# Strided PV between the local transposes, shared V rows and a result copy on ScalarE, and half sums of layer 1 among local PV

## The chip, the cores and the metric

One core of one Trainium2 chip. The metric is device time in microseconds (us). A profile of one execution goes with each kernel; its span starts a little later than the timed interval, so 332.4 in the trace belongs to 334.2 timed. Engines: PE (TensorE, matmuls), PEld (its weight loads), DVE (VectorE), ACT (ScalarE), POOL (GpSimd).

## The reference

```python
# attention: batch 8, heads 8, seq 576, head_dim 64
mask_local   = (rel >= 0) & (rel < 32)                          # heads 0-3
mask_strided = (rel >= 0) & (pos[None, :] % 32 == pos[:, None] % 32)   # heads 4-7
attn = softmax(where(mask, q @ k.T / 8, -1e9)); attn_out = attn @ v
x = attn_out.transpose(0, 2, 1, 3).reshape(4608, 512)
h = x @ w_in                                                    # 512 -> 2048, "layer 1"
g = maximum(h, 0) + alpha * minimum(h, 0)
out = g @ w_out                                                 # 2048 -> 512, "layer 2"
```

## The kernel before

The heads are handled in pairs: two strided and two local pairs per batch. For each unit of two pairs, `T` transposes q or k on PE and copies the result on DVE and ACT; `Sc` makes scores and their exponentials (ACT); `Pv` multiplies by V, takes a reciprocal and a product on DVE; `X` transposes the result and copies it to `xT`, layer 1's input. Layer 1 makes 16 blocks of 128 columns per 512 tokens; each block is 4 matmuls into a buffer in PSUM, the memory that matmuls write to (3 buffers in turn), a negative part on ACT and `gT` on DVE, which frees the buffer. Batches 0 and 1 are fed first, in a fixed order; batch 0 alone, with filler matmuls on a zero tile between pieces, meant to keep the PE clock up, batch 1 between pieces of layer 2.

```python
    def over_v(b, eng):                      # the 32 V rows that neighbouring blocks share
        v16 = vls[b % 2]
        cast_copy(eng, v16[0:32, 1:24, :], v16[96:128, 0:23, :])

    def alone(u0, u1, ahead):                # u0: strided unit, u1: local unit
        A, L = (2 * u0, 2 * u0 + 1), (2 * u1, 2 * u1 + 1)
        # ... T(u0,q) T(u0,k), four Sc of A, T(u1,q) T(u1,k), two Sc of L[0],
        #     six Pv of A, two Sc of L[1], X(A[0]) X(A[1]),
        #     over_v on DVE, four Pv of L, X(L[0]) X(L[1])        (cut to its order)

    def lin1_piece(n, m):
        # ...
        hps = phpool.tile([128, 512], F32, tag="hps", name="hps")
        for kk in range(4):                  # kk 0, 1: local pairs; kk 2, 3: strided pairs
            # ... matmul(hps, win16[:, kk, block m], xT[:, kk, tokens])
        neg = npool.tile([128, 512], F32, tag="neg", name="neg")
        keep(nc.scalar.activation(neg, hps, AF.Relu, scale=-1.0))
        def fin():
            keep(nc.vector.scalar_tensor_tensor(
                gTs[n][:, m, :], neg, oma[:, m : m + 1], hps, op0=ALU.mult, op1=ALU.add))
        late.append(fin)
```

The softmax here doesn't subtract the row's maximum and nothing guards it: scores larger than these inputs give would overflow.

Of the kernel before, what the change touches and what calls it, by code (L numbers as in the profile page):

```python
# [9 lines left out]
F32 = mybir.dt.float32  # L10
# [21 lines left out]
def kernel(  # L32
# [10 lines left out]
    nc = tc.nc  # L43
    keep = tc.keep_in_program_order

    B, H, S, D = q.shape
# [17 lines left out]
    phpool = ctx.enter_context(tc.tile_pool(name="ph", bufs=3, space=bass.MemoryType.PSUM))  # L64
    pbpool = ctx.enter_context(tc.tile_pool(name="pb", bufs=1, space=bass.MemoryType.PSUM))
# [4 lines left out]
            name=nc.get_next_instruction_name(), act_func_set_id=6, ins=[], outs=[]  # L70
# [10 lines left out]
    win16 = cpool.tile([128, 4, 2048], F16)  # L81
    wout16 = cpool.tile([128, 16, 512], F16)
    xT = cpool.tile([128, 4, RING], F16)
# [89 lines left out]
    def cast_copy(eng, o, i):  # L173
        if eng == "act":
            keep(nc.scalar.copy(o, i))  # L175
        elif eng == "dve":
            keep(nc.vector.tensor_copy(o, i))  # L177
        else:
            keep(nc.gpsimd.tensor_copy(o, i))  # L179

    def cast_v(b, pr, eng):

        v16 = vss[b % 2]
        cast_copy(eng, v16[0:72, 2 * pr : 2 * pr + 2, :, 0:64],
                  loaded[b][0:72, 1024 * pr : 1024 * pr + 1024].rearrange(
                      "p (h t d) -> p h t d", h=2, t=8))
        cast16[(b, True, "v")] = v16

    def over_v(b, eng):

        v16 = vls[b % 2]
        cast_copy(eng, v16[0:32, 1:24, :], v16[96:128, 0:23, :])
# [7 lines left out]
    NEARLY = 2  # L200

    def make_pair(g):
        P = Pair()
        P.g, P.b, P.hp = g, g // 4, g % 4
        P.strided = P.hp >= 2
        P.pr = P.hp % 2
        P.n, P.w = (8, 72) if P.strided else (6, 96)
        u = g // 2
        P.dx = P.b >= DX and P.strided
        P.xd = P.b >= DX and P.hp < 3  # L210
        if P.dx:
            P.qT, P.kT = (z[u % 2].rearrange("r e c -> r (e c)") for z in (qTs, kTs))
        else:
            P.qT, P.kT = qTs[u % 2][:, g % 2], kTs[u % 2][:, g % 2]
        P.sgroups = ([0, 1, 2, 3], [4, 5, 6, 7]) if P.strided else ([0, 1, 2], [3, 4, 5])
        P.pgroups = ([0, 1, 2], [3, 4, 5], [6, 7]) if P.strided else P.sgroups
        P.et = {}
        P.x16 = None
        return P
# [111 lines left out]
    def pv_piece(P, a):  # L331
        if P.x16 is None:
            if P.xd and P.strided:
                P.x16 = x16s
            else:
                P.x16 = xpool.tile([128, 1024], F16, tag="x16", name="x16")
        v16 = cast16[(P.b, P.strided, "v")]
        grp = P.pgroups[a]
        r = 72 if P.strided else 128
        pv = pspool.tile([128, 512], F32, tag="ps", name="pv")  # L340
        nb = 2 * len(grp)
        for x in range(nb):
            t, hh = grp[x // 2], x % 2
            et, c = P.et[(t, hh)]
            keep(nc.tensor.matmul(  # L345
                pv[:, 65 * x : 65 * x + 65], et[0:r, c : c + 128],
                v16[0:r, 2 * P.pr + hh, t, :] if P.strided else v16[:, 6 * (2 * P.pr + hh) + t, :],
                start=(x == 0), stop=(x == nb - 1), skip_group_check=True))
        w = P.w
        rc = rpool.tile([128, 8], F32, tag="rc", name="rc")  # L350
        pvv = pv[0:w, 0 : 65 * nb].rearrange("r (c e) -> r c e", e=65)
        keep(nc.vector.reciprocal(rc[0:w, 0:nb], pvv[:, :, 64]))  # L352
        c0 = 128 * grp[0]
        keep(nc.vector.tensor_tensor(  # L354
            P.x16[0:w, c0 : c0 + 64 * nb].rearrange("r (c e) -> r c e", e=64),
            pvv[:, :, 0:64],
            rc[0:w, 0:nb].unsqueeze(2).to_broadcast([w, nb, 64]), op=ALU.mult))

    def x_piece(P):
        xp = pspool.tile([128, 1024], F16, tag="ps", name="xp")  # L360
        for t in range(P.n):
            keep(nc.tensor.transpose(  # L362
                xp[:, P.w * t : P.w * t + P.w], P.x16[0 : P.w, 128 * t : 128 * t + 128], ident[0 : P.w, 0 : P.w]))
        base = (P.b % 4) * S
        if P.strided:
            keep(nc.scalar.copy(  # L366
                xT[:, P.hp, base : base + S].rearrange("r (p t) -> r p t", t=8),
                xp[:, 0:576].rearrange("r (t p) -> r p t", t=8)))
        else:
            keep(nc.vector.tensor_copy(xT[:, P.hp, base : base + S], xp[:, 0:576]))  # L370

    def x_dma(P):
        base = (P.b % 4) * S
# [14 lines left out]
    pairs = [make_pair(g) for g in range(npair)]  # L388
    pieces = []

    def feed(fn, g):
        pieces.append((g, fn))

    def T(u, nm):
        return lambda: transpose_piece(u, nm)

    def Sc(g, i):
        return lambda: score_piece(pairs[g], i)

    def Pv(g, i):  # L400
        return lambda: pv_piece(pairs[g], i)

    def X(g):
        return lambda: x_piece(pairs[g])

    def alone(u0, u1, ahead):

        A, L = (2 * u0, 2 * u0 + 1), (2 * u1, 2 * u1 + 1)
        feed(T(u0, "q"), -1)
        feed(T(u0, "k"), -1)  # L410
        for g in A:
            for i in range(2):
                feed(Sc(g, i), -1)
        if ahead:
            feed(T(u1, "q"), -1)
            feed(T(u1, "k"), -1)
            for i in range(2):
                feed(Sc(L[0], i), -1)
        for g in A:
            for i in range(3):  # L420
                feed(Pv(g, i), -1)
        if not ahead:
            feed(T(u1, "q"), -1)
            feed(X(A[0]), -1)
            feed(T(u1, "k"), -1)
            feed(X(A[1]), -1)
            for i in range(2):
                feed(Sc(L[0], i), -1)
        for i in range(2):
            feed(Sc(L[1], i), -1)  # L430
        if ahead:
            for g in A:
                feed(X(g), -1)
        for g in L:
            for i in range(2):
                if g == L[0] and i == 0:
                    feed(lambda: (over_v(u0 // 2, "dve"), pv_piece(pairs[L[0]], 0)), -1)
                else:
                    feed(Pv(g, i), -1)
        for g in L:  # L440
            feed(X(g), -1)

    alone(1, 0, True)
    end0 = len(pieces)
    alone(3, 2, True)
    end1 = len(pieces)


# [75 lines left out]
    def attn_step(end):  # L524
        if pos["i"] < end:
            pieces[pos["i"]][1]()
            pos["i"] += 1
        while late:
            late.pop(0)()


    gTs = {}

    def lin1_piece(n, m):
        if m == 0:
            gTs[n] = gpool.tile([128, 16, 512], F16, tag="gT", name="gT")
        c0 = (512 * n) % RING
        parts = [(c0, 0, min(512, RING - c0))]
        if c0 + 512 > RING:
            parts.append((0, RING - c0, 512 - (RING - c0)))  # L540
        hps = phpool.tile([128, 512], F32, tag="hps", name="hps")
        for kk in range(4):
            for x, (src, dst, w) in enumerate(parts):
                keep(nc.tensor.matmul(  # L544
                    hps[:, dst : dst + w],
                    win16[:, kk, 128 * m : 128 * m + 128],
                    xT[:, kk, src : src + w],
                    start=(kk == 0 and x == 0),
                    stop=(kk == 3 and x == len(parts) - 1),
                    skip_group_check=True,  # L550
# [9 lines that stand above are left out]
# [45 lines left out]
    def warm(n):  # L605

        for _ in range(n):
            keep(nc.tensor.matmul(wps, wrm[:, 0:128], wrm, start=True, stop=True))  # L608
# [54 lines left out]
    for i in range(end0):  # L663
        if i == 1:
            keep(nc.tensor.transpose(apt[:, 0:16], alpha_r, id16))
            keep(nc.vector.tensor_scalar(
                oma, apt[:, 0:16], -1.0, 1.0, op0=ALU.mult, op1=ALU.add))
        if i == 4:
            cast_v(0, 0, "dve")
            cast_v(0, 1, "dve")  # L670
        attn_step(end0)
        if i < 2:
            warm(4)
        else:
            warm(1)

    def attn_n(n, end):
# [78 lines left out]
```

## Time and profile before

| | before |
|---|---|
| time, median (lowest to highest of 6) | 334.18 us (333.87 to 334.32) |
| first local PV on PE, batch 0 / batch 1 | 23.02 / 61.38 us |
| layer 1 resumes after batch 0 / batch 1 (both inputs there) | 27.16 / 66.59 us |
| layer 1 of the first tokens ends, layer 2 begins | 40.75 us |
| copy of the shared V rows | DVE, 0.54 us |

Times in the middle rows are positions in the trace. The prediction shows the lines they come from. PE is 96% busy, so what counts is when PE gets its next input. The two handovers from attention to layer 1 are the places where it has to wait.

### The profile page before, as it was taken

The page shows a single profiled execution, that of the slowest core. Times are in us where ns is not written, and L with a number is a line of the kernel's source. Part 1 is how long each engine was busy: PE and PEld are TensorE (multiplying, and loading weights), DVE is VectorE, ACT ScalarE, POOL GpSimd, SP SyncE. Part 2 cuts the span into 40 slices and gives each one's busy share as a digit, 9 for nine tenths or more (in the row PEclk, how much of TensorE's full clock was granted, in tenths as well). Part 3 has the DMA queues.
Part 4 walks back from the last instruction along what each step waited for, and adds up shares of the span by engine and source line. Part 5 has one row for each costly group of instructions (what it writes and reads, how often), then busy time and mean ns, then how long its engine had stood idle before and what let it go on. Part 6 is the DMA issues. An engine that isn't in the chain of part 4 may idle for free.

```text
span 332.4 us, 6351 instructions
## 1 busy us (share of the span) xinstructions
PE 320.5 (96%) x2533; PEld 163.2 (49%) x2533; DVE 185.1 (56%) x363; ACT 172.5 (52%) x300; POOL 142.2 (43%) x154
## 2 busy tenths in 40 slices
PE   6899999999999999999999999999999999999995
PEld 2554455554554444444558754445444444444444
DVE  5477836477553873387428833784368337605800
ACT  2644753467535744575457644773476336425611
POOL 7932497137679365736483528332611400000000
PEclk9999999999999999999999999999999999999999
DMA  6999999399398649683979295715530120011011
GB/s 220 191 207 207 236 210 194 85 245 157 66 87 125 200 59 147 114 234 40 154 138 221 25 153 109 133 13 109 129 67 20 49 85 33 0 65 63 0 63 65
DMA packets 73117, 39.22 MB, mean 118 GB/s; under 512 B 54064, under 2 KB 64768, under 8 KB 73088
## 3 DMA queue, kind: packets, MB, share of 16 engines
q0 software_dynamic: 41760, 17.38, 48.7%
q1 hardware_dynamic: 31328, 21.44, 26.0%
q8 instruction: 20, 0.33, 0.4%
q14 instruction: 9, 0.07, 0.1%
HBM read 38.01 MB, written 9.44 MB: 143 GB/s over the span
## 4 chain that ended last, share of the span: by engine, by line
PE 89%; DVE 4%; ACT 3%; DMA 2%; issue 1%; SPq 0%; ACTq 0%
PE ops L586 37%; PE hps L544 36%; PE pv L345 4%; PE sp L295 4%; PE tp L235 3%; DMA ql<-in_q_dram 2%; DVE x L354 1%; PE wps L608 1%; PE ops L577 1%; ACT xT L366 1%; DVE qT L177 1%; ACT osb L591 1%; PE sp L311 1%; PE sph L311 1%; PE xp L362 1%
## 5 line engine op out<-in xcount | busy, mean ns | idle before, releaser
L586 PE MATMUL ops<-wout,gT 128*128 128x512 f16 x560 | 136.9, 379 | 0.2 <-DVE gT L557 0.2
L544 PE MATMUL hps<-xT,win 128*128 128x512 f16 (+1 forms) x640 | 134.3, 358 | 2.5 <-ACT xT L366 2.0
L557 DVE SCALAR_TENSOR_TENSOR gT<-neg,oma,hps 128x512 f16<-128x512 f32 x144 | 106.0, 744 | 49.8 <-ACT neg L554 42.2
L554 ACT ACTIVATE neg<-hps 128x512 f32<-128x512 f32 x144 | 86.0, 597 | 46.4 <-PE hps L544 45.2
L329 POOL TENSOR_TENSOR et<-et,consts 128x576 f16<-128x576 f16 (+1 forms) x48 | 61.1, 1274 | 95.4 <-ACT et L319 95.3
L544 PEld LDWEIGHTS <-win 128*128 128x128 f16 x640 | 59.4, 98 | 59.4 <-issue 6.1
L586 PEld LDWEIGHTS <-gT 128*128 128x128 f16 x560 | 48.3, 97 | 46.3 <-issue 0.5
L319 ACT ACTIVATE et<-sp 72x576 f16<-72x576 f32 (+1 forms) x56 | 36.1, 645 | 29.2 <-PE sp L295 15.3
L591 ACT COPY osb<-ops 128x512 f32<-128x512 f32 x35 | 20.5, 585 | 53.4 <-PE ops L586 49.6
L352 DVE RECIPROCAL rc<-pv 72x6 f32<-72x6 f32 (+2 forms) x80 | 14.9, 186 | 55.7 <-PE pv L345 55.6
L354 DVE TENSOR_TENSOR x<-pv,rc 96x384 f16<-96x384 f32 (+2 forms) x65 | 34.5, 531 | 2.2
L345 PEld LDWEIGHTS <-et 72*128 72x128 f16 (+1 forms) x448 | 23.4, 98 | 16.5 <-DVE x L354 1.1
L295 PEld LDWEIGHTS <-kT 64*128 64x128 f16 x448 | 10.8, 95 | 26.5 <-issue 21.2
L295 PE MATMUL sp<-qT,kT 64*128 64x72 f16 (+1 forms) x392 | 16.9, 201 | 1.9 <-ACT kT L175 1.7
L177 DVE COPY qT<-tp 128x1024 f16<-128x1024 f16 (+1 forms) x11 | 11.3, 1030 | 12.3 <-PE tp L235 12.3
L608 PE MATMUL wps<-wrm 128*128 128x512 f16 x44 | 15.7, 428 | 1.2 <-DVE wrm L620 1.2
L167 POOL DMA_DIRECT2D vl<-in_v_dram x8 | 11.1, 1394 | 10.7 <-PE xp L362 9.1
L345 PE MATMUL pv<-vs,et 72*128 72x65 f16 x256 | 15.3, 194 | 0.1
L179 POOL COPY vs<-stv 72x1024 f16<-72x1024 f16 x14 | 14.3, 1032 | 0.0
L175 ACT COPY kT<-tp 128x1024 f16<-128x1024 f16 (+1 forms) x11 | 9.4, 858 | 8.4 <-PE tp L235 8.4
L345 PE MATMUL pv<-vl,et 128*128 128x65 f16 x192 | 11.1, 194 | 0.0
L383 ACT COPY xT<-xs 128x576 f16<-128x576 f16 x5 | 6.5, 1301 | 5.2 <-DMA xs<-x16s 5.2
(73 smaller groups left out, 169.5 us busy)
## 6 DMA issues: line engine op xcount, KB each, us to landing
out_dram<-osb SPq DMA_DIRECT2D x35, 256.0 KB, 2.3
ql<-in_q_dram SPq DMA_DIRECT2D x6, 512.0 KB, 5.5
kl<-in_k_dram SPq DMA_DIRECT2D x6, 512.0 KB, 6.6
stv<-in_v_dram POOLq DMA_DIRECT2D x8, 288.0 KB, 6.2
vl<-in_v_dram POOLq DMA_DIRECT2D x6, 384.0 KB, 9.8
win<-in_moe_w_in_dram POOLq DMA_DIRECT2D x4, 512.0 KB, 10.1
wout<-in_moe_w_out_dram POOLq DMA_DIRECT2D x4, 512.0 KB, 17.1
ql<-in_q_dram POOLq DMA_DIRECT2D x3, 512.0 KB, 8.9
```

Source lines behind the costliest of these rows:

```text
L295: keep(nc.tensor.matmul(sps[y][:, w * x : w * x + w], P.kT[hf, k0 : k0 + 128], P.qT[hf, q0 : q0 + w], start=(x == 0), stop=(x == len(grp) ...
L319: keep(nc.scalar.activation(ev.rearrange("r (y c) -> r y c", y=2), sp[0:r, :, 0:n], AF.Exp, scale=SCALE))
L329: keep(nc.gpsimd.tensor_tensor(ev, ev, m, op=ALU.mult))
L345: keep(nc.tensor.matmul(pv[:, 65 * x : 65 * x + 65], et[0:r, c : c + 128], v16[0:r, 2 * P.pr + hh, t, :] if P.strided else v16[:, 6 * (2 * ...
L352: keep(nc.vector.reciprocal(rc[0:w, 0:nb], pvv[:, :, 64]))
L354: keep(nc.vector.tensor_tensor(P.x16[0:w, c0 : c0 + 64 * nb].rearrange("r (c e) -> r c e", e=64), pvv[:, :, 0:64], rc[0:w, 0:nb].unsqueeze ...
L544: keep(nc.tensor.matmul(hps[:, dst : dst + w], win16[:, kk, 128 * m : 128 * m + 128], xT[:, kk, src : src + w], start=(kk == 0 and x == 0) ...
L554: keep(nc.scalar.activation(neg, hps, AF.Relu, scale=-1.0))
L557: keep(nc.vector.scalar_tensor_tensor(gTs[n][:, m, :], neg, oma[:, m : m + 1], hps, op0=ALU.mult, op1=ALU.add))
L586: keep(nc.tensor.matmul(ops, gTs[n][:, kf, 128 * mt : 128 * mt + 128], wout16[:, kf, :], start=(kf == 0), stop=(kf == 15)))
L591: keep(nc.scalar.copy(osb, ops))
L608: keep(nc.tensor.matmul(wps, wrm[:, 0:128], wrm, start=True, stop=True))
```

## The change

Its intent, read from the diff: fill the wait for the local transposes with strided PV; relieve DVE, which works without pause before the local part, by giving ACT the V rows and one result copy; and replace filler by useful work, the kk 2 and 3 halves of five layer 1 blocks ("half sums" below).

```diff
-            keep(nc.vector.tensor_copy(xT[:, P.hp, base : base + S], xp[:, 0:576]))
+            cast_copy("act" if P.b < NEARLY and P.hp == 0 else "dve",
+                      xT[:, P.hp, base : base + S], xp[:, 0:576])
 ...
+        fns += [Pv(A[0], 0), T(u1, "q"), Pv(A[0], 1), T(u1, "k"), Pv(A[0], 2), Sc(L[0], 0), Sc(L[0], 1)]
+        fns += [Pv(A[1], 0), Pv(A[1], 1), Sc(L[1], 0), Pv(A[1], 2), Sc(L[1], 1), X(A[0]), X(A[1])]
+        fns += [lambda: (over_v(u0 // 2, "act"), pv_piece(pairs[L[0]], 0)), Pv(L[0], 1)]
+        fns += pre[0:2] + [Pv(L[1], 0)] + pre[2:3] + [Pv(L[1], 1)] + pre[3:] + [X(L[0]), X(L[1])]
 ...
+    def lin1_pre(m):
+        if m == 3:
+            sp = pbpool.tile([128, 2, 512], F32, tag="sp", name="hps4")
+            pre[3], pre[4] = sp[:, 0], sp[:, 1]
+        else:
+            pre[m] = phpool.tile([128, 512], F32, tag="hps", name="hps")
+        for z in ((3, 4) if m == 3 else (m,)):
+            for kk in (2, 3):
+                keep(nc.tensor.matmul(pre[z], ..., start=(kk == 2), stop=False, ...))
 ...   # lin1_piece: where a half sum is ready, only kk 0 and 1 are added;
 ...   # filler stops once half sums have begun (both cut)
```

More of the change, by code (lines that the diff above doesn't have):

```diff
@@ L404, in X, with alone @@
         return lambda: x_piece(pairs[g])
-    def alone(u0, u1, ahead):
+    def alone(u0, u1, pre):
         A, L = (2 * u0, 2 * u0 + 1), (2 * u1, 2 * u1 + 1)
-        feed(T(u0, "q"), -1)
-        feed(T(u0, "k"), -1)
-        for g in A:
-            for i in range(2):
-                feed(Sc(g, i), -1)
-        if ahead:
-            feed(T(u1, "q"), -1)
-            feed(T(u1, "k"), -1)
-            for i in range(2):
-                feed(Sc(L[0], i), -1)
-        for g in A:
-            for i in range(3):
-                feed(Pv(g, i), -1)
-        if not ahead:
-            feed(T(u1, "q"), -1)
-            feed(X(A[0]), -1)
-            feed(T(u1, "k"), -1)
-            feed(X(A[1]), -1)
-            for i in range(2):
-                feed(Sc(L[0], i), -1)
-        for i in range(2):
-            feed(Sc(L[1], i), -1)
-        if ahead:
-            for g in A:
-                feed(X(g), -1)
-        for g in L:
-            for i in range(2):
-                if g == L[0] and i == 0:
-                    feed(lambda: (over_v(u0 // 2, "dve"), pv_piece(pairs[L[0]], 0)), -1)
-                else:
-                    feed(Pv(g, i), -1)
-        for g in L:
-            feed(X(g), -1)
-    alone(1, 0, True)
+        fns = [T(u0, "q"), T(u0, "k")] + [Sc(g, i) for g in A for i in range(2)]
+        fns += [Pv(A[0], 0), T(u1, "q"), Pv(A[0], 1), T(u1, "k"), Pv(A[0], 2), Sc(L[0], 0), Sc(L[0], 1)]
+        fns += [Pv(A[1], 0), Pv(A[1], 1), Sc(L[1], 0), Pv(A[1], 2), Sc(L[1], 1), X(A[0]), X(A[1])]
+        fns += [lambda: (over_v(u0 // 2, "act"), pv_piece(pairs[L[0]], 0)), Pv(L[0], 1)]
+        fns += pre[0:2] + [Pv(L[1], 0)] + pre[2:3] + [Pv(L[1], 1)] + pre[3:] + [X(L[0]), X(L[1])]
+        for fn in fns:
+            feed(fn, -1)
+    alone(1, 0, [lambda m=m: lin1_pre(m) for m in range(4)])
     end0 = len(pieces)
-    alone(3, 2, True)
+    alone(3, 2, [])
     end1 = len(pieces)
@@ L532 @@
     gTs = {}
+    pre = {}
+    def lin1_pre(m):
[6 more added lines that the diff above has]
+            for kk in (2, 3):
+                keep(nc.tensor.matmul(
+                    pre[z], win16[:, kk, 128 * z : 128 * z + 128], xT[:, kk, 0:512],
+                    start=(kk == 2), stop=False, skip_group_check=True))
     def lin1_piece(n, m):
@@ L540, in lin1_piece @@
             parts.append((0, RING - c0, 512 - (RING - c0)))
-        hps = phpool.tile([128, 512], F32, tag="hps", name="hps")
-        for kk in range(4):
+        ready = n == 0 and m in pre
+        hps = pre[m] if ready else phpool.tile([128, 512], F32, tag="hps", name="hps")
+        if ready:
+            for z in ((3, 4) if m == 3 else () if m == 4 else (m,)):
+                for kk in (0, 1):
+                    keep(nc.tensor.matmul(
+                        pre[z], win16[:, kk, 128 * z : 128 * z + 128], xT[:, kk, 0:512],
+                        start=False, stop=(kk == 1), skip_group_check=True))
+        for kk in () if ready else range(4):
             for x, (src, dst, w) in enumerate(parts):
@@ L673 @@
             warm(4)
-        else:
+        elif not pre:
             warm(1)
```

## The prediction

> **What bounds the kernel now.** I read the page first (busy shares, chain of waits), then the busy time by stage, then the chain in order of time, then the timelines of PE, ACT and DVE up to 66 us, since the change touches nothing later.
>
> ```profile
> PE 320.5 (96%) x2533; PEld 163.2 (49%) x2533; DVE 185.1 (56%) x363; ACT 172.5 (52%) x300; POOL 142.2 (43%) x154
> ...
> PE 89%; DVE 4%; ACT 3%; DMA 2%; issue 1%; SPq 0%; ACTq 0%
> ```
>
> PE is the bound: 96% busy and 89% of the chain. The rest of the chain lies mostly in the attention of batches 0 and 1, where PE hands over to DVE and ACT and back. By stage (stretch in us, its length, then busy time of each engine with instruction counts):
>
> ```profile
> 13.50:26.67 13.17, 11.61 (x157) 6.85 (x156) 9.20 (x27) 5.75 (x13) 6.14 (x12) 1.00 1.43 193
> 26.67:40.75 14.08, 13.97 (x66) 6.24 (x64) 10.93 (x16) 8.96 (x15) 4.45 (x7) 1.00 1.24 217
> 40.75:66.10 25.35, 23.96 (x259) 13.39 (x258) 12.33 (x32) 11.66 (x26) 15.92 (x20) 1.00 1.25 167
> 66.10:105.20 39.10, 38.69 (x351) 19.92 (x351) 24.43 (x48) 22.44 (x40) 26.67 (x27) 1.00 0.85 138
> ```
>
> Stage A (13.5 to 26.7) is batch 0's attention; much of its PE time is filler on a zero tile, so 11.61 busy is no bound there. Stage B (26.7 to 40.75) is layer 1 of the first tokens, 64 matmuls back to back. Stage C (to 66.1) is batch 1's attention threaded into layer 2. From 66 us on PE is 99% busy (38.69 of 39.10), so a microsecond gained or lost before 66 us should reach the end unchanged. The chain (start, length, what):
>
> ```profile
> 25.69 0.56 DVE x L354
> 26.64 0.47 DVE xT L370
> 27.16 13.76 PE hps L544 x63
> 40.91 1.73 PE ops L586 x8
> ...
> 65.13 0.56 DVE x L354
> 66.08 0.47 DVE xT L370
> 66.59 5.12 PE hps L544 x23
> ```
>
> A and C both end on the same hand-over: normalise the last local PV, transpose it, copy xT, and only then layer 1 resumes, at 27.16 and 66.59. These two times are what the change must pull in. What precedes the first, on DVE and ACT (start, length, instruction, idle before):
>
> ```profile
> 22.00 0.54 DVE L177 COPY vl<-vl 32x1495 f16<-32x1495 f16 x1
> 23.40 0.19 DVE L352 RECIPROCAL rc<-pv 96x6 f32<-96x6 f32 x1 [0.85 <-PE pv L345]
> ...
> 21.98 0.71 ACT L316 ACTIVATE et<-sph 128x288 f16<-128x288 f32 x2
> 22.57 1.19 ACT L366 COPY xT<-xp 128x576 f16<-128x576 f16 x2
> 28.00 0.60 ACT L554 ACTIVATE neg<-hps 128x512 f32<-128x512 f32 x1 [4.24 <-PE hps L544]
> ```
>
> The V rows shared between blocks cost 0.54 us on DVE and are ready at 22.54, before local PV starts on PE (23.02). ACT then idles 4.24 us, which is the slack the change aims at. But ACT comes free for that work only about 23.7, after exponentials and two xT copies.
>
> **What the Trainium skill says.** (1) "ScalarE: Activation LUTs", section "What ACT_TABLE_LOAD costs": an ACTIVATE with immediate scale and bias takes 186 ns + 0.833 ns per element, and neighbours overlap by about 93 ns. The trace agrees for copies too: kT 128x512 590 ns, the 128x1024 cast 1045 ns (the formula gives 613 and 1039). For the 1495 columns of V I estimate 0.186 + 1495 x 0.000833 = 1.43 us. (2) The same page's "Rules for kernel authors" calls VectorE up to about 3x faster per element on 16-bit single-source work; the trace has 0.54 on DVE, so 2.6x by this estimate. (3) "PSUM — Partial Sum Buffer", section "PSUM bank collisions raise a hardware error": two engines must not touch one bank in the same quadrant at once, and by bank is the simple guard. In the trace ACT's copy of one half of tp starts only when DVE's copy of the other half has ended (14.29 + 0.69, then 15.01). (4) "TensorE: Matmul & The Clock Gate", Part 1: PE falls to half clock after an idle window of about 3.4 us. The trace has clock 1.00 throughout these stages, and its longest PE pause there is 0.90 us.
>
> **The change part by part.** I walk each engine's queue of the changed program in order with durations and starts of the old trace. Steps used: strided PV of 6 matmuls to its reciprocal 0.38 (17.65 to 18.03), reciprocal plus product 0.70 (18.03 to 18.73), filler 0.22, score piece 0.49, eight transposes 0.45, 128x512 matmul 0.216 (13.76 / 63 is 0.218), about 0.05 from a finish to its waiter.
>
> *Strided PV between the local transposes.* Old: six strided PVs from 17.65, and DVE works without pause from 18.03 to 22.54. New: the first PV goes at 13.64, right after the strided scores, and fills DVE's and ACT's wait for the local transposes. The price: the transposes' copies alternate with the products on DVE (x 14.25, qT 14.72, then ACT's qT 15.45, kT 15.93 to 16.52), so local scores start at 16.84, not 16.14. Then PVs and scores alternate at PE's own pace: local scores 16.84, 17.64, 19.24, 20.38; strided transposes 21.09 and 21.57; the first local PV stands at PE's head at 22.05 instead of 23.02. Gain 0.97.
>
> *V rows on ACT.* In ACT's queue this copy stands behind the last exponential (21.06 to 21.77) and both xT copies (21.65 to 22.84). It starts near 22.72 and ends near 24.15. The first matmul of local PV doesn't need it, the second does: 24.2. PE stands 2.1 us. Gain of 0.97 has become a loss of 1.18 (24.2 against 23.02).
>
> *Half sums of five blocks.* Ten matmuls (2.16 us) move out of stage B to between the four local PVs, where filler stood. They also spread the PVs: 24.2, 24.57, 25.83, 26.44. The last product ends at 27.69, the last transposes end at PE 28.0, xT of the first local pair is on ACT (27.93 to 28.5) beside DVE's (28.19 to 28.66). Layer 1's second halves start at 28.55 and have both inputs at about 28.77, against 27.16: 1.61 late, less the 2.16 already done.
>
> *What follows in stage B.* Five blocks are complete 2.16 us after the start, while ACT (0.60) and then DVE (0.75, pitch about 0.67) take them one by one: gT 0 starts 29.80, then 30.47, 31.14, 31.81 (ends 32.56). Blocks 3 and 4 share one two-bank tile, and in the changed program ACT's negative part of block 4 waits for DVE's gT of block 3, although they lie in two banks. So block 4 goes 32.59 on ACT, 33.22 on DVE, gT 5 from 33.89 to 34.64. PE has blocks 5, 6, 7 done at 33.3, and block 8 needs the buffer of block 5: it starts 34.69, a stop of 1.4. Blocks 8 to 15 take 8 x 0.864 = 6.9: end 41.6 instead of 40.75. Sum up to here: 1.61 - 2.16 + 1.4 = +0.85.
>
> *Stage C*, on the old clock. The order is the same without half sums. The interleaving saves the two pauses around the local transposes (old 0.47 before the scores at 51.58) and little else: the first local PV stands ready at 61.15, not 61.38. But ACT's queue there is xT (59.35 to 59.95), the layer 2 result copy (60.2 to 60.8), xT (to 61.3), V rows (61.2 to 62.65). PE stands from 61.15 to 62.7. Three layer 2 pieces and PVs later the last PV is at 65.8; old it was at 64.52 with layer 1 resuming 2.07 later. So 67.87 instead of 66.59: +1.28.
>
> Sum: 0.85 + 1.28 = +2.1 us, so 334.2 + 2.1 = 336.3.
>
> **The rivals.** (a) *The intended gain.* If V rows were ready by 22.0 and 61.1 (ACT's copy cheap, or its queue earlier than I walk), stage A would end 2.1 sooner and C 1.5 sooner: about 332.7. For it: ACT idles 4.24 us there in total. Against: the queue order puts exponentials and xT copies ahead, and nothing at 1495 columns on ACT can be near 0.5 us when 512 take 0.59. (b) *Nothing shows:* the half sums give 2.16 and the wait on ACT takes it, with DVE keeping up in stage B: without the 1.4 stop the time is 334.9. For it: DVE is busy only 10.93 of 14.08 there. Against: in bursts it isn't the average that counts, with three buffers. (c) *The clock.* Filler ends once half sums begin, and PE has pauses of 2.1, 1.4 and 1.5 us. If that were idle enough to halve the clock for a window, another 1.7 to 3.4 would be lost: 338 to 340. Against: each pause is under 3.4 us.
>
> **Range and chances.** Most of my error is in the two waits for V rows (1.43 us is estimated, no such copy ran on ACT) and in the stop in stage B. Halving both V waits gives 334.5, all of them longer by 0.5 with a spell of lower clock gives 338.5. Range 334.0 to 338.3. Two per cent is 6.7 us, more than any sum of these: faster 0.01, within 0.96, slower 0.03.
>
> **What would show each step.** Right: ACT's vl copy at 1.4 us, ending near 24.2 and near 63.5 (62.65 plus the 0.85); PE idle before PV on vl of about 2 and 1.5 us, released by ACT; layer 1's second halves from about 28.6; block 4's ACT step starting after block 3's gT; PE waiting over 1 us for a gT near 33 to 35; layer 1 of the next tokens resuming near 68.7. Wrong: a vl copy under 0.9 us, local PV starting before 23 us, no PE idle among the layer 1 blocks, or PE clock below 1.00 in stages A to C.

## The result and the profile after

The changed kernel took 336.65 us (median of 6, 336.41 to 338.34) against 334.18: ratio 1.0081, 95% interval 1.0061 to 1.0102, so 0.8% slower. Ratios here are the mean time of one kernel's fast runs over that of the other's of the same rounds, so not quite the ratio of the medians.

PE of the changed kernel in batch 0 and layer 1 (start, length, instruction, count, and the idle time before it with what ended it):

```profile
22.06 0.19 PE L345 MATMUL pv<-vl,et 128*128 128x65 f16 x1
24.32 0.31 PE L345 MATMUL pv<-vl,et 128*128 128x65 f16 x5 [2.06 <-ACT vl L175]
...
28.75 2.32 PE L536 MATMUL hps<-xT,win 128*128 128x512 f16 x10 [0.47 <-ACT xT L175]
30.91 2.75 PE L541 MATMUL hps<-xT,win 128*128 128x512 f16 x12
34.85 7.07 PE L541 MATMUL hps<-xT,win 128*128 128x512 f16 x32 [1.19 <-DVE gT L554]
41.76 1.89 PE L583 MATMUL ops<-wout,gT 128*128 128x512 f16 x8
```

Local PV arrives 0.96 us earlier than before (22.06 against 23.02) and is then stopped after one matmul. The second matmul is the first that reads the shared rows, and it waits for ACT. Later PE stops once more, between the block 7 and block 8 matmuls, for a gT. ACT in the same kernel shows why the rows are late:

```profile
21.02 0.71 ACT L316 ACTIVATE et<-sph 128x288 f16<-128x288 f32 x2 [0.37 <-PE sph L311]
21.62 1.19 ACT L366 COPY xT<-xp 128x576 f16<-128x576 f16 x2
22.83 1.43 ACT L175 COPY vl<-vl 32x1495 f16<-32x1495 f16 x1
...
31.11 0.60 ACT L551 ACTIVATE neg<-hps 128x512 f32<-128x512 f32 x1 [0.15 <-PE hps L536]
32.77 2.07 ACT L551 ACTIVATE neg<-hps 128x512 f32<-128x512 f32 x4 [1.06 <-DVE gT L554]
...
61.30 0.59 ACT L588 COPY osb<-ops 128x512 f32<-128x512 f32 x1 [0.23 <-PE ops L583]
61.78 0.65 ACT L366 COPY xT<-xp 128x576 f16<-128x576 f16 x1
62.31 1.43 ACT L175 COPY vl<-vl 32x1495 f16<-32x1495 f16 x1
```

The V copy takes 1.43 us, and it starts only when the exponential and two xT copies ahead of it are through. In batch 1 a layer 2 result copy stands ahead too. Begun that late, the copy's length counts nearly in full: it starts 0.58 us after PE's first matmul ended (22.06 + 0.19) in batch 0, and 0.10 before that in batch 1 (62.22 + 0.19), so 1.43 of the first pause and all of the second are the copy itself. The line at 32.77 is block 4's negative part, which waited 1.06 us for block 3's gT; the two blocks are the two halves of one tile, `hps4`. DVE, in turn, waited for it:

```profile
30.01 2.72 DVE L554 SCALAR_TENSOR_TENSOR gT<-neg,oma,hps 128x512 f16<-128x512 f32 x4 [1.24 <-ACT neg L551]
33.40 2.72 DVE L554 SCALAR_TENSOR_TENSOR gT<-neg,oma,hps 128x512 f16<-128x512 f32 x4 [0.66 <-ACT neg L551]
```

PE in batch 1 of the changed kernel:

```profile
62.22 0.19 PE L345 MATMUL pv<-vl,et 128*128 128x65 f16 x1
63.79 0.31 PE L345 MATMUL pv<-vl,et 128*128 128x65 f16 x5 [1.37 <-ACT vl L175]
...
68.97 3.40 PE L541 MATMUL hps<-xT,win 128*128 128x512 f16 x15 [0.28 <-DVE xT L177]
```

Layer 1 resumes at 68.97 instead of 66.59, which is 2.38 late; the span is 334.8 instead of 332.4, which is 2.4 longer. So everything was lost before 69 us and nothing after. The page of the whole execution sums the two pauses in one row (busy time, mean ns of one, idle before and its releaser), first before, then after:

```profile
L345 PE MATMUL pv<-vl,et 128*128 128x65 f16 x192 | 11.1, 194 | 0.0
```

```profile
L345 PE MATMUL pv<-vl,et 128*128 128x65 f16 x192 | 11.4, 194 | 3.4 <-ACT vl L175 3.4
```

### The profile page after: what moved, and what is told of

Read it like the earlier page. It is cut to its first block, busy times and chain, and to the rows that moved or that the text cites. A ratio compares the mean times of both kernels' runs of the same rounds, so it can differ in the third digit from the quotient of the medians.

```text
span 334.8 us, 6345 instructions
## 1 busy us (share of the span) xinstructions
PE 320.1 (96%) x2529; PEld 163.8 (49%) x2529; DVE 183.4 (55%) x359; ACT 176.2 (53%) x304; POOL 142.1 (42%) x154
## 4 chain that ended last, share of the span: by engine, by line
PE 75%; ACT 3%; DVE 2%; issue 1%; ACTq 0%
PE ops L583 34%; PE hps L541 32%; PE pv L345 3%; PE sp L295 3%; PE tp L235 2%; PE ops L574 1%; ACT xT L366 1%; ACT osb L588 1%; DVE gT L554 1%; ACT vl L175 0%; DVE qT L177 0%; DVE x L354 0%; PE xp L362 0%; ACT neg L551 0%; PE tt L263 0%
## 5 line engine op out<-in xcount | busy, mean ns | idle before, releaser
L541 PE MATMUL hps<-xT,win 128*128 128x512 f16 (+1 forms) x620 | 130.0, 357 | 3.6 <-ACT xT L366 2.0
L541 PEld LDWEIGHTS <-win 128*128 128x128 f16 x620 | 57.5, 98 | 58.2 <-issue 7.2
L345 PEld LDWEIGHTS <-et 72*128 72x128 f16 (+1 forms) x448 | 24.3, 98 | 20.4 <-issue 3.6
L605 PE MATMUL wps<-wrm 128*128 128x512 f16 x40 | 14.9, 455 | 1.2 <-DVE wrm L617 1.2
```

Of the source, the lines that this page charges most:

```text
L345: keep(nc.tensor.matmul(pv[:, 65 * x : 65 * x + 65], et[0:r, c : c + 128], v16[0:r, 2 * P.pr + hh, t, :] if P.strided else v16[:, 6 * (2 * ...
L541: keep(nc.tensor.matmul(hps[:, dst : dst + w], win16[:, kk, 128 * m : 128 * m + 128], xT[:, kk, src : src + w], start=(kk == 0 and x == 0) ...
L605: keep(nc.tensor.matmul(wps, wrm[:, 0:128], wrm, start=True, stop=True))
```

## The experiments

The main theory: PE stands for the V rows because of their place in ACT's queue (2.06 and 1.37 us), and part of the half sums' gain is lost to a stop of layer 1 for a buffer. The rivals: the new order of PV itself delays the local part; DVE or ACT is overloaded as a whole; the PE clock drops. All kernels gave correct results. Three groups ran on three chips, each with runs of the kernel before in the same rounds (medians 334.16, 334.22, 334.16).

| run | us, median (range) | ratio to before (95% interval) |
|---|---|---|
| e1 V rows on DVE | 332.75 (332.43 to 332.99) | 0.9957 (0.9945 to 0.9969) |
| e2 V rows on ACT, earlier | 332.92 (332.64 to 333.04) | 0.9962 (0.9950 to 0.9974) |
| e3 no half sums | 337.44 (336.93 to 337.67) | 1.0101 (1.0087 to 1.0116) |
| e4 block 4's negative part early | 337.62 (336.12 to 337.93) | 1.0093 (1.0076 to 1.0110) |
| e5 before, V rows on ACT | 338.11 (337.97 to 338.54) | 1.0118 (1.0105 to 1.0132) |
| e6 before, new order alone | 333.10 (332.97 to 333.13) | 0.9966 (0.9953 to 0.9980) |
| e7 e1 and e4 together | 332.28 (332.21 to 332.41) | 0.9943 (0.9930 to 0.9955) |
| e8 e4 with filler in the pause | 336.14 (336.11 to 336.31) | 1.0058 (1.0046 to 1.0071) |
| e9 e1 with four half sums | 332.04 (331.66 to 332.37) | 0.9933 (0.9920 to 0.9947) |
| e10 e7, result copy on DVE | 332.59 (332.29 to 332.69) | 0.9950 (0.9938 to 0.9963) |
| e11 e4 again | 336.15 (336.06 to 336.48) | 1.0062 (1.0049 to 1.0074) |
| e12 e8 again | 336.07 (336.06 to 336.16) | 1.0057 (1.0044 to 1.0070) |

All lie within 2% of before. The intervals separate kernels with the late V rows from those without; among e1, e2, e6, e7, e9 and e10 they overlap in part, and differences there lean on the traces.

### e1: V rows back on DVE

```diff
-        fns += [lambda: (over_v(u0 // 2, "act"), pv_piece(pairs[L[0]], 0)), Pv(L[0], 1)]
+        fns += [lambda: (over_v(u0 // 2, "dve"), pv_piece(pairs[L[0]], 0)), Pv(L[0], 1)]
```

> The changed kernel with only the copy of the shared V rows back on DVE. Theory A (PE stood for that copy in ACT's queue, 2.06 us in batch 0 and 1.37 us in batch 1): both pauses go, everything behind them moves up, time 336.65 - 2.2 - 1.5 = 332.9, below the kernel before (334.2). DVE is idle there (3.75 and 4.79 us before the first local reciprocal), so the 0.54 us copy should not show on it. Rival B (the new order of strided PV and local transposes itself delays the local part, and the V rows only fill that delay): under 1 us is won, 335.7 or more. Rival C (DVE becomes the bound again, as the change's author feared): 335 to 336, with a new DVE wait before local PV.

Measured 332.75, 3.9 below the changed kernel and 1.4 below before. The V copy on DVE and PE of this kernel:

```profile
20.94 0.54 DVE L177 COPY vl<-vl 32x1495 f16<-32x1495 f16 x1
...
22.06 0.34 PE L345 MATMUL pv<-vl,et 128*128 128x65 f16 x6
...
26.53 2.32 PE L536 MATMUL hps<-xT,win 128*128 128x512 f16 x10 [0.47 <-ACT xT L175]
28.68 2.75 PE L541 MATMUL hps<-xT,win 128*128 128x512 f16 x12
32.64 7.07 PE L541 MATMUL hps<-xT,win 128*128 128x512 f16 x32 [1.20 <-DVE gT L554]
...
65.22 5.12 PE L541 MATMUL hps<-xT,win 128*128 128x512 f16 x23 [0.27 <-DVE xT L177]
```

The six matmuls run through, and all that follows is 2.2 us earlier; the stop at block 8 is unchanged, so it is a cost of its own. The copy took its 0.54 us on DVE at 20.94, ahead of need. After batch 1 layer 1 resumes at 65.22 instead of 68.97, 3.75 earlier, and the two profiled runs differ by 3.76 (336.69 and 332.93). Rivals B and C fall.

### e2: V rows on ACT, but earlier in its queue

```diff
-... Pv(A[1], 0), Pv(A[1], 1), ... lambda: (over_v(u0 // 2, "act"), pv_piece(pairs[L[0]], 0)) ...
+... lambda: (pv_piece(pairs[A[1]], 0), over_v(u0 // 2, "act")), Pv(A[1], 1), ... Pv(L[0], 0) ...
```

> The changed kernel with the V rows still on ACT, but issued earlier in ACT's queue: behind the first strided PV of the second pair, where ACT is idle from 18.92 to 20.00 and from 56.5 to 57.8. Theory A (the place in the queue costs, not the engine or its 1.43 us): as on DVE, 332.9 to 333.3, no PE pause before local PV, perhaps 0.2 us of delay of one exponential. Rival (ACT's total load is what costs, since ACT got 3.7 us more work): no gain, about 336.6.

Measured 332.92, as on DVE. ACT of this kernel:

```profile
18.64 1.43 ACT L175 COPY vl<-vl 32x1495 f16<-32x1495 f16 x1
19.98 0.64 ACT L319 ACTIVATE et<-sp 128x576 f16<-128x576 f32 x1
```

The same 1.43 us on the same engine, ended by 20.1. So in a good place neither the engine nor the length costs anything. The place is what made the 1.43 us count: emitted at its consumer, the copy sits behind everything that ACT was given before. What a shorter copy would cost in that late place was not run.

### e3: no half sums

```diff
-    alone(1, 0, [lambda m=m: lin1_pre(m) for m in range(4)])
+    alone(1, 0, [])
```

> The changed kernel without the half sums of layer 1 (filler stays in their place; V rows and one result copy still on ACT). Theory A: the 2.16 us of PE work moved ahead is nearly all given back, because the half sums spread the local PVs (layer 1's start moves from about 28.9 to 28.4 without them) and because layer 1 then stops 1.2 us for a buffer; layer 1 would end near 42.05 instead of 41.76, so the time is 336.9 (336.6 to 337.2), and there is no stop among the layer 1 blocks. Rival (the half sums are worth their 2.16 us): 338.5 or more. Second rival (they cost on balance): 336.2 or less.

The median is 337.44, above the range I gave. Three of the four runs had a mean clock of 0.994 or 0.995; the fourth, profiled, had 0.998 and took 336.93, as expected. Its PE:

```profile
27.94 14.25 PE L541 MATMUL hps<-xT,win 128*128 128x512 f16 x64
42.02 1.89 PE L583 MATMUL ops<-wout,gT 128*128 128x512 f16 x8
```

64 matmuls without a stop end at 42.02; with the half sums layer 1 ended at 41.76. So ten matmuls moved ahead, 2.16 us of work, gained 0.26 us there. The rest was given back where the prediction put it, in a later start (28.75 against 27.94) and in the stop for a buffer (1.19).

### e4: the negative parts of blocks 3 and 4 together

```diff
+        if ready and m == 4:
+            return
+        both = []
+        for z in ((3, 4) if ready and m == 3 else (m,)):
             neg = npool.tile([128, 512], F32, tag="neg", name="neg")
-            keep(nc.scalar.activation(neg, hps, AF.Relu, scale=-1.0))
+            keep(nc.scalar.activation(neg, pre[z] if ready else hps, AF.Relu, scale=-1.0))
+            both.append(...)      # fin() then makes both gT
```

> The changed kernel with the negative parts of blocks 3 and 4, which share one two-bank tile, both taken on ACT before DVE's two gT, so that no gT stands between them. Theory A (the stop of 1.19 us at block 8 comes in part from block 4's ACT step waiting for block 3's gT, which leaves DVE idle 0.66 us): DVE's idle 0.66 falls to about 0.2 (block 3's gT now waits for both negative parts), the stop falls to about 0.7, time 336.15 (335.9 to 336.3). Rival (the stop comes from DVE's pace alone, four gT at 0.68 against blocks that PE finishes at 0.43): unchanged, 336.65.

The mechanism came out as expected. DVE and PE of this kernel:

```profile
32.14 3.38 DVE L561 SCALAR_TENSOR_TENSOR gT<-neg,oma,hps 128x512 f16<-128x512 f32 x5 [0.15 <-ACT neg L556]
```

```profile
34.26 7.07 PE L541 MATMUL hps<-xT,win 128*128 128x512 f16 x32 [0.68 <-DVE gT L561]
```

DVE's 0.66 fell to 0.15, PE's 1.19 to 0.68, and the profiled run took 336.12. But the median of the six runs is 337.62: two runs at 0.998 and 0.999 of the clock took 336.37 and 336.12, four at 0.994 took 337.60 to 337.93. The changed kernel itself had one such run among six, 338.34 at 0.994. The same kernel run again on another chip (e11) had none and took 336.15, 0.5 under the changed kernel, as expected here.

### e5: the kernel before with V rows on ACT alone

```diff
-                    feed(lambda: (over_v(u0 // 2, "dve"), pv_piece(pairs[L[0]], 0)), -1)
+                    feed(lambda: (over_v(u0 // 2, "act"), pv_piece(pairs[L[0]], 0)), -1)
```

> The kernel before with only the copy of the shared V rows moved to ACT. Theory A (the copy's place in ACT's queue, behind exponentials and two xT copies, costs in the old order too): it runs on ACT from about 23.8 to 25.2 and from 61.5 to 62.9, local PV waits to 25.3 instead of 23.02 and to 63.0 instead of 61.38, so 334.2 + 2.3 + 1.6 = 338.1; some runs may be 1 to 2 us longer at a clock of 0.994, as three kernels with such a pause showed. Rival (the wait comes only from the new order of PVs): 334.2, DVE then being relieved of 0.54 us in its busiest stretch, or 333.7.

Measured 338.11. PE of this kernel, batch 0 and batch 1:

```profile
25.41 0.31 PE L345 MATMUL pv<-vl,et 128*128 128x65 f16 x5 [2.07 <-ACT vl L175]
```

```profile
65.32 0.31 PE L345 MATMUL pv<-vl,et 128*128 128x65 f16 x5 [1.37 <-ACT vl L175]
```

The pauses of the changed kernel, nearly to the hundredth, in the old order. One word of the diff is worth +3.9 us here, as it was worth 3.9 in e1.

### e6: the new order alone

```diff
 # the new list of pieces on the kernel before; over_v on "dve", both xT copies on DVE, pre = []
```

> The kernel before with only the new order of strided PV between the local transposes (V rows and both result copies on DVE, no half sums). Theory A: local PV starts at 22.06 instead of 23.02 and DVE's chain of four reciprocals and products moves up as a whole, and 0.17 us is won in batch 1: 334.2 - 0.96 - 0.17 = 333.05. Rival (the alternation with the products delays local scores by 0.70 us, and this is what stays): 334.2 or more.

Measured 333.10: 1.1 us won, as worked out. Local PV began at 21.96.

### e7: both mends

```diff
 # the diffs of e1 and e4 on the changed kernel
```

> The changed kernel with both mends: V rows on DVE, and the negative parts of blocks 3 and 4 taken together ahead of the two gT. Theory A: the two costs are apart in time, so their gains add: 332.75 - 0.55 = 332.2. Rival (with the earlier start the stop at block 8 is bound by something else, a weight transfer for instance): 332.75, unchanged.

Measured 332.28, as if the two gains add, though e1's and e7's intervals touch. The trace agrees: the stop is 0.68 where e1 has 1.20.

```profile
32.23 7.07 PE L541 MATMUL hps<-xT,win 128*128 128x512 f16 x32 [0.68 <-DVE gT L561]
```

### e8, e11 and e12: the pause and the clock

```diff
# on e4's kernel; e11 is e4's kernel as it was, e12 is this one again
-lambda: (over_v(u0 // 2, "act"), pv_piece(pairs[L[0]], 0))
+lambda: (over_v(u0 // 2, "act"), warm(9) if u0 == 1 else None, pv_piece(pairs[L[0]], 0))
```

> As e4 (V rows on ACT, block 4's negative part early), with nine matmuls on the zero tile in PE's pause of 2.06 us in batch 0; they end near 24.0, before the copy does, so no instruction is held up. Four of six runs of e4 took 337.6 to 337.9 us at a mean clock of 0.994 and two took 336.1 and 336.4 at 0.998 and 0.999. Theory (PE's pause lets its clock drop for a while in some runs): all runs at 0.998 or more, 336.1 to 336.4. Rival (the drop comes from the chip or from load elsewhere in the kernel, not from this pause): the same mixture, with runs at 337.6.

> The kernel of e4 again, beside e12 on the same chip in the same rounds, for the clock alone. Theory (PE's pause of 2.07 us lets the clock drop in some runs): some of the runs at a mean clock near 0.994 and 337.6 us, the rest near 0.999 and 336.2. Rival (the spell of e4 was the chip's at that time): all at 336.2.

> The kernel of e8 again, in the same rounds as e11. Theory: no run below 0.998, all near 336.2. Rival: the same share of runs near 0.994 and 337.6 as e11.

PE of e8 shows that the filler took the pause of batch 0; local PV then runs once the V rows are there:

```profile
21.95 2.33 PE L612 MATMUL wps<-wrm 128*128 128x512 f16 x10
24.11 0.63 PE L345 MATMUL pv<-vl,et 128*128 128x65 f16 x6
```

With filler all five runs of e8 were at 0.998 or more, 336.11 to 336.31. On a third chip e4's kernel (e11) and the one with filler (e12) ran in the same rounds, and neither showed a low run, meaning one at a mean clock of 0.994 or 0.995: 336.06 to 336.48 and 336.06 to 336.16, all at 0.998 or more. So the direct comparison decided nothing. Over all runs: kernels with the pause of 2.06 us had 9 low runs of 25, kernels without it none of 40, nor did the 29 runs of before whose clock is on record. That is an association. It holds on one chip by itself: seven of the nine are runs of e3 and e4 (7 of 10), and e1, e2 and before had none of 21 in those rounds. No profiled run was a low one, so where in the kernel the clock fell isn't shown, and the low run of e5 (338.54) was only some 0.5 us longer than its fellows. What the pause does to the clock stays open.

### e9: half sums of four blocks

```diff
-            pre[3], pre[4] = sp[:, 0], sp[:, 1]
+            pre[3] = sp[:, 0]
 # and z runs over (m,) alone in both places; V rows on DVE
```

> The changed kernel with V rows on DVE and half sums of four blocks instead of five, so that no two blocks share the two-bank tile and no guard stands between blocks 3 and 4. Theory A (five blocks overfill the three buffers; with four the stop in layer 1 shrinks from 1.20 to about 0.45 in all, layer 1 starts 0.3 earlier, two matmuls more remain): 332.75 - 0.76 = 332.0, as good as or slightly better than e7. Rival (each block taken out of the half sums costs its 0.43 us): 333.2.

Measured 332.04, the fastest median of all, 2.1 us under before; its interval overlaps that of e7. PE and, from the chain of work of its profiled run (332.37, its slowest), one piece (start, length, what):

```profile
28.29 10.56 PE L541 MATMUL hps<-xT,win 128*128 128x512 f16 x48 [0.17 <-DVE gT L554]
38.69 1.89 PE L583 MATMUL ops<-wout,gT 128*128 128x512 f16 x8
```

```profile
135.60 8.18 DMA kT<-ksd
```

The only stop for a buffer that is left is 0.17, now before block 4, instead of 1.20 before block 8. Layer 1 ends at 38.69, against 39.54 in e1, although two more matmuls are left for it. In that run the chain contains a DMA transpose that the other chains I read lack; PE waited 0.24 us for it, in this one place.

### e10: the result copy back on DVE

```diff
-            cast_copy("act" if P.b < NEARLY and P.hp == 0 else "dve",
+            cast_copy("dve",
```

> As e7 (both mends) with the one result copy (xT of the first local pair) back on DVE as well. Theory A: in e1 ACT's copy ended at 26.48 and DVE's at 26.55, each waited for on its own; on DVE the first copy can start when the last product ends (25.5) and ends about 25.97, the second goes 26.09 to 26.55 as now, so layer 1 starts no later, perhaps 0.15 earlier: 332.1 to 332.3. Rival (the intent of the change: two copies in turn on DVE delay the second by 0.47): 332.75, and again 0.47 in batch 1, up to 333.2.

Measured 332.59, ratio 0.9950 where e7 had 0.9943; the intervals overlap. Neither 332.1 to 332.3 nor 332.75 and more is hit. In the trace the first layer 1 matmul starts earlier, at 26.24 against 26.64 in e7, of which 0.2 is there before local PV, and the matmuls behind the second halves start at 28.54 against 28.79, so almost nothing is left of it; batch 1 shows nothing either way. So this part of the change is worth at most some 0.3 us, with its sign unsettled.

## Why the prediction was right

The predicted time, 336.3, is 0.35 under the measured median. By its own steps:

- **PV between the transposes.** First local PV predicted at PE's head at 22.05, measured 22.06; alone it wins 1.1 us (e6).
- **V rows on ACT.** The estimate of 1.43 us was the measured 1.43. End near 24.15 predicted, 24.26 measured (22.83 + 1.43). The walk let the copy begin 0.12 before the xT copies end, as it did in batch 1 (62.31 against 61.78 + 0.65); in batch 0 it began when they had ended (21.62 + 1.19), for a reason that isn't shown. The pause of 2.1 was 2.06. e1, e2 and e5 show that it is this, and that it comes from the place in the queue.
- **Half sums.** Second halves predicted from 28.55, measured 28.75. Of these 0.20, 0.12 was there when the V rows came (24.32 against 24.2), and 0.07 is the xT copy on ACT, taken as 0.57 us and measured 0.64.
- **The stop in layer 1.** Block 8 predicted at 34.69, measured 34.85; the guard between blocks 3 and 4 is shown by e4 (0.66 to 0.15 on DVE). My 1.4 counts from the issue of the last matmul, the 1.19 in the trace from its modelled end. End of layer 1: 41.6 predicted, 41.76 measured, so +1.01 and not +0.85.
- **Stage C.** +1.28 predicted; measured 2.38 - 1.01 = 1.37. V rows ended at 63.74 (62.31 + 1.43), predicted 63.5; my pause of 1.55 counts from the start of the first matmul, and so counted it is 1.57 (62.22 to 63.79); the 1.37 in the trace counts from its modelled end.
- **After 66 us nothing is won back:** 2.38 at 68.97, 2.4 at the end of the span. The stages missed by 0.16 and 0.09, both in the same direction, so the hit does not rest on stage errors that cancel.

Rival (a) is not what happened, since the rows came late: they cost 3.9 us on ACT in that place (e1, e5). But its number, about 332.7 if the rows were ready in time, is what e1 (332.75) and e2 (332.92) measured. Rival (b) fails: DVE did not keep up, PE stopped 1.19 us for a gT, and the half sums gained 0.26 in the trace (e3) and not 2.16. Rival (c) I judged too lightly: the profiled run has clock 0.999, yet one of six runs of the changed kernel took 338.34 at 0.994, just outside my range, and its cause is open.

The parts of the change, across chips: order -1.1 (e6), half sums with the result copy -0.35 (e1 less e6), V rows on ACT +3.9 (changed less e1), together +2.45; measured 336.65 - 334.18 = +2.47. That is no check, since each step starts from the median where the last one ended, so that they must sum to nearly the whole. The check is e5, where the V rows alone cost +3.9 in the old order. The -0.35 is not resolved by the times (the intervals of e1 and e6 overlap).

## What to carry to other kernels

Idle time on an engine is only worth something at the moment when the work is due. Here ACT worked its queue in order, so a copy emitted at its consumer waited for all that was emitted before it (begun at 22.83, and at 18.64 when emitted earlier); move it ahead in the queue before you move it to another engine. And work pulled forward on the bounding engine comes back as a wait if the engine that drains its buffers can't take the burst: five half sums gained 0.26 us of 2.16. Four did better than five as first written (e9 against e1); part of that is the tile that blocks 3 and 4 shared (0.5 us, e4), and four against five with this mended (e7) is not resolved.

## What the Trainium skill lacked or had wrong

- "ScalarE: Activation LUTs", "Rules for kernel authors": the table gives a factor of about 3 between the engines for bf16 and lists no plain copy. The same fp16 copy of 1495 columns took 1.43 us on ACT and 0.54 us on DVE, a factor of 2.6.
- "TensorE: Matmul & The Clock Gate" names idle windows of about 3.4 us (Part 1) as what lowers the clock; its section on psum-queue depth-cycling adds frequent short idles between groups of matmuls, without a length. Neither says what one shorter pause does. Kernels with the pause of 2.06 us ran at a mean clock of 0.994 or 0.995 in 9 of 25 runs, the others in 0 of 40. The link isn't proved here; whether a pause of this length is safe stays open.
- "PSUM — Partial Sum Buffer" speaks of guarding by bank. The built program guards by tile: of two blocks in two banks of one tile one waited for the other, 0.66 us on DVE, 0.15 once both ACT steps went first (e4). No page that I read says how a tile that spans two banks is guarded.
- "TensorE: Matmul & The Clock Gate" says in passing that ACT's and DVE's queues are strict FIFO; no page that I read draws the rule: a copy given to an engine with idle time is still late if it is emitted behind other work (PE waited 2.06 and 1.37 us for it, and not at all once it was emitted earlier).
